# A searched instruction order keeps less of the source's order at its front

## The chip, the core and the metric

One core of a Trainium2 chip runs the program. The time is the device time of one execution in microseconds (us); lower is better. A core has five engines with an instruction queue each, which they work through in order: TensorE (PE in the profile; PEld are its weight loads), VectorE (DVE), ScalarE (ACT), GpSimd (POOL) and SyncE (SP), which here issues nearly all DMAs. The engines wait for each other by semaphores.

## What is computed

```python
xn = layernorm(x)                      # x: 1 x 2048 x 512
qkv = xn @ wqkv                        # 32 heads of 16
pq, pk = phi(q), phi(k)                # phi(t) = where(t > 0, t + 1, exp(t)) + 1e-6
kv = einsum("bhsd,bhse->bhde", pk, v); z = einsum("bhsd->bhd", pk)
o = einsum("bhqd,bhde->bhqe", pq, kv) / (einsum("bhqd,bhd->bhq", pq, z)[..., None] + 1e-6)
h = relu(xn @ w1 + b1) ** 2            # 1376 hidden columns
out = x + o @ wo + (h @ w2 + b2)       # float32
```

## The kernel before

The 2048 rows are 16 token tiles of 128 rows. A first loop over the tiles normalises each (xp), transposes it (PE for tiles 0 to 7, DVE after an exchange by DMA for the others), splits it into two parts whose sum is the float32 value (h and l: xs0h, xs0l for the transposed columns, tok for the rows), multiplies it with the k columns of wqkv (project, weights wkh and wkl), applies phi (k, then pk, again in two parts) and adds pk and the rows into four PSUM banks (kx). The names in the profile are those tiles, with their buffer numbers left out: st, mv and y are the statistics of the layernorm, t a transposed tile kept for DRAM. All later products are made of three passes of such parts.

After that two rounds (n = 0, 1) run over two blocks of 512 rows each. In each a loop makes the products with the columns of wqkv and w1 by a scheme of seven products instead of eight on half blocks (sums T of the rows, operands ops of the weights), evicts the PSUM banks (tiles rr, rf, h, more, by ACT copies and DVE additions), and then the second products with w2 and wo follow, whose left operands s are split by ACT and DVE just ahead. The operands of the weights are made in the first round from raw rows (raw), stored in DRAM (wd) and reloaded. At the end DVE transposes the results, adds them to x (res) and they are stored. There are four PSUM banks named ps and four named acc.

No instruction goes to an engine in the order of the source directly. A recorder (class Program) takes them as a list of 3188 tasks with their dependences. `order`, before anything is built, decides each engine's order by a search over its own cost table, and `emit` then writes the instructions out in the order of the planned starts. All instructions are written out at one line, L349, which is why the profile shows it for each.

Three lines set what the search may move. In `order`, an engine's fixed lane holds all of TensorE's tasks and, for other engines, those with an index below `nc.fixed`:

```python
self.lanes = {e: [t for t in ts if t.engine == e and (e == "tensor" or t.index < self.fixed)] for e in self.ENGINES}
...
for start in self.STARTS:
    chance, back = random.Random(start), (8, 16, 4)[start % 3]
```

A fixed lane is played in the source's order. After it, an engine takes of the tasks that are ready the one with the earliest due time. Each of the two starts in `STARTS` seeds a random generator; in 500 rounds the due times of tasks that led up to a planned TensorE wait are moved forward by random shares of it (`press`), the plan is played again, and the best is kept; `back` is after how many rounds without a gain the search returns to its best. The two results are then mixed by stretches of time. In the kernel's body `nc.fixed` is set after the recording of tiles 0 to 2's projections and of the first kx:

```python
kx(0)
nc.fixed = len(nc.tasks)
for i in range(2, NT):
```

The list holds 170 tasks at this point, the matmuls among them counted.

Of the kernel before, what the change touches and what calls it, by code (L numbers as in the profile page):

```python
# [79 lines left out]
class Program:  # L80
# [96 lines left out]

    ENGINES = ("tensor", "vector", "scalar", "gpsimd", "sync")
    DEEP, FAR = 4.0, 15.0
    STARTS = (6, 14)  # L180
    ROUNDS = 500

    def order(self):
# [36 lines left out]
        plain, best, found = [t.due for t in ts], None, []  # L220
        for start in self.STARTS:
            chance, back = random.Random(start), (8, 16, 4)[start % 3]
# [138 lines left out]
def kernel(  # L361
# [12 lines left out]
    nc = Program(tc.nc)  # L374
# [466 lines left out]
    def kx(i):  # L841
        order = (((1, 0),), ((0, 0), (0, 1))) if i >= NPE else (((0, 0),), ((0, 1),), ((1, 0),))
        todo = [(c, u, v) for group in order for c in range(NJ) for u, v in group]
        first, last = order[0][0], order[-1][-1]
        for c, u, v in todo:
            nc.tensor.matmul(kxp[c], lhsT=tok[i][:, u, c * P:(c + 1) * P], rhs=pk[i][:, v],
                             start=i == 0 and (u, v) == first, stop=i == NT - 1 and (u, v) == last)
# [394 lines left out]

    kxp = [bank(f"kx{c}", "acc") for c in range(NJ)]
    kx(0)
    nc.fixed = len(nc.tasks)
    for i in range(2, NT):
        if i == 3:
            nc.sync.dma_start(b1s[:, :NF - 1], b1[:(NF - 1) * P].rearrange("(f p) -> p f", p=P))
# [471 lines left out]
```

## Time and profile before

| | |
|---|---|
| median of 3 runs | 401.57 us (401.56 to 401.84) |
| profiled execution | 402.07 us |
| its span (first to last instruction) | 400.4 us |
| PE busy | 392.6 us, 98% |
| DVE, ACT, POOL busy | 353.5, 271.7, 49.5 us |
| granted TensorE clock | 0.997 of full |
| DMA | 94.37 MB, mean 236 GB/s |

The times of the stretches below are taken in the profiled execution, from its span's start. PE's matmuls are pipelined and their ends modelled in the profile, so "busy" can hide short gaps; a row of the timeline gives start, length, engine, line, operation, tiles out<-in, shapes, and in brackets the idle time of the engine just before with what ended it.

### The profile page before, as it was taken

Reading aid. Unit: us, or ns where it says so; the run is one execution under the profiler, and the core shown is the slowest. Engines: PE = TensorE matmul, PEld = TensorE weight load, DVE = VectorE, ACT = ScalarE, POOL = GpSimd, SP = SyncE. Lnnn points to the kernel's source line nnn. Section 1 sums busy time; section 2 is a strip of 40 time slices with the busy share of each in tenths; the row PEclk is TensorE's granted clock in tenths of the full one; section 3 lists DMA queues with packets and bytes.
Section 4 is the critical chain, followed back from the end, with each engine's and each line's share of the span. In section 5 each row is a group of like instructions: output and inputs, shape, how many; then the busy total and the mean of one; then the engine's idle time right before and its main releaser. Section 6 shows DMA issues by size and latency. Waiting matters only on the chain.

```text
span 400.4 us, 5611 instructions
## 1 busy us (share of the span) xinstructions
PE 392.6 (98%) x1763; PEld 324.5 (81%) x1763; DVE 353.5 (88%) x577; ACT 271.7 (68%) x478; POOL 49.5 (12%) x68
## 2 busy tenths in 40 slices
PE   7999999999999999999999999999999999999994
PEld 6778888888888887888888888887888888888884
DVE  5899999999998998999999999879999679676884
ACT  5786777677778989999757553186867677455440
POOL 2232322320122444100000000000000000000000
PEclk9999999999999999999999999999999999999998
DMA  7872387979678997797545799999975589999434
GB/s 235 289 220 58 94 249 229 338 283 310 248 230 306 327 359 275 250 315 262 186 146 199 245 235 243 306 250 255 272 232 185 178 226 292 227 281 278 156 64 95
DMA packets 80770, 94.37 MB, mean 236 GB/s; under 512 B 39490, under 2 KB 50754, under 8 KB 80484
## 3 DMA queue, kind: packets, MB, share of 16 engines
q1 hardware_dynamic: 79556, 93.49, 76.2%
q10 hardware_dynamic: 1088, 0.26, 0.3%
q0 software_dynamic: 96, 0.26, 0.3%
q8 instruction: 14, 0.23, 0.2%
q14 instruction: 16, 0.13, 0.1%
HBM read 57.81 MB, written 34.08 MB: 230 GB/s over the span
## 4 chain that ended last, share of the span: by engine, by line
PE 59%; DVE 1%; issue 0%
PE ps L349 32%; PE acc L349 28%; DVE res L349 0%; DVE o L349 0%
## 5 line engine op out<-in xcount | busy, mean ns | idle before, releaser
L349 PE MATMUL ps<-s,ops 128*128 128x512 f32 x435 | 102.6, 390 | 0.0
L349 PEld LDWEIGHTS ps<-s,ops 128*128 128x128 f32 x435 | 81.6, 188 | 17.1 <-ACT s L349 0.3
L349 DVE TENSOR_TENSOR s<-rr,s 128x512 fp32r<-128x512 f32 x56 | 38.2, 690 | 13.5 <-ACT s L349 12.9
L349 ACT ACTIVATE s<-rr 128x512 fp32r<-128x512 f32 x56 | 34.9, 630 | 22.2 <-DVE s L349 10.2
L349 PE MATMUL acc<-s,ops 128*128 128x512 f32 (+1 forms) x210 | 47.9, 380 | 0.0
L349 PE MATMUL acc<-pk,tok 128*128 128x512 f32 x192 | 47.1, 394 | 0.0
L349 PEld LDWEIGHTS acc<-s,ops 128*128 128x128 f32 x210 | 38.3, 188 | 7.5
L349 PEld LDWEIGHTS acc<-pk,tok 128*128 128x128 f32 x192 | 35.5, 188 | 7.8 <-DVE pk L349 0.6
L349 PE MATMUL acc<-T,ops 128*128 128x512 f32 x168 | 41.3, 390 | 0.0
L349 PE MATMUL ps<-T,ops 128*128 128x512 f32 x168 | 40.9, 391 | 0.1
L349 PEld LDWEIGHTS acc<-T,ops 128*128 128x128 f32 x168 | 31.5, 188 | 6.9 <-ACT rr L349 0.4
L349 PEld LDWEIGHTS ps<-T,ops 128*128 128x128 f32 x168 | 31.4, 188 | 7.0 <-ACT rf L349 0.5
L349 POOL DMA_DIRECT2D out_dram<-res x2 | 1.5, 728 | 229.0 <-DVE res L349 226.4
L349 POOL TENSOR_TENSOR tok<-xp,tok 128x512 fp32r<-128x512 f32 x16 | 21.7, 1354 | 42.1 <-ACT tok L349 30.6
L349 PE MATMUL ps<-xs0h,ops 128*128 128x512 f32 x72 | 23.7, 390 | 0.0
L349 ACT ACTIVATE rr<-acc 128x512 f32<-128x512 f32 x23 | 13.4, 586 | 12.3 <-PE acc L349 12.3
L349 DVE STREAM_TRANSPOSE d<-d 128x1024 f32<-128x1024 f32 x16 | 19.8, 1240 | 1.7 <-ACT d L349 1.5
L349 POOL TENSOR_TENSOR ops<-s,ops 128x512 fp32r<-128x512 f32 x12 | 15.9, 1328 | 25.3 <-ACT ops L349 22.2
L349 PE MATMUL acc<-xs0h,ops 128*128 128x512 f32 x56 | 18.4, 390 | 0.0
L349 ACT ACTIVATE s<-rf 128x512 fp32r<-128x512 f32 x19 | 11.9, 629 | 8.4 <-DVE rf L349 4.9
L349 ACT ACTIVATE rr<-rr,odds 128x512 f32<-128x512 f32 x15 | 10.8, 721 | 9.7 <-DVE rr L349 9.5
L349 DVE TENSOR_TENSOR ops<-raw,ops 128x512 fp32r<-128x512 f32 (+1 forms) x22 | 15.0, 681 | 2.6 <-ACT ops L349 2.6
(169 smaller groups left out, 801.4 us busy)
## 6 DMA issues: line engine op xcount, KB each, us to landing
ops<-wd SPq DMA_DIRECT2D x84, 256.0 KB, 4.1
wd<-ops SPq DMA_DIRECT2D x35, 512.0 KB, 3.6
ops<-wd SPq DMA_DIRECT2D x21, 512.0 KB, 5.8
wd<-ops SPq DMA_DIRECT2D x28, 256.0 KB, 3.5
res<-in_A_x_dram SPq DMA_DIRECT2D x32, 128.0 KB, 6.5
out_dram<-res SPq DMA_DIRECT2D x26, 128.0 KB, 3.6
ops<-wdz SPq DMA_DIRECT2D x6, 512.0 KB, 6.2
x<-in_A_x_dram SPq DMA_DIRECT2D x5, 512.0 KB, 4.9
```

What stands on the lines that cost most here:

```text
L349: getattr(getattr(self.nc, t.engine), t.name)(*map(real, t.args), **{k: real(a) for k, a in t.kw.items()})
```

## The change

`nc.fixed` becomes the constant 140. The tasks 140 to 169 of the list no longer keep the source's order: 12 of them are matmuls, which do so anyhow, and 18 belong to DVE (10), ACT (5), POOL (1) and SP (2). They are the end of the work on tiles 0 to 2: the roots and the normalisation of tile 3, phi and the parts of k of tile 1, the rows tok of tile 1, the statistics of tiles 8 and 9, and the loads of two raw blocks of w2. Besides, the two starts of the search are 0 and 9 instead of 6 and 14, with 8 and 8 as `back` instead of 8 and 4. Since both feed the search, the order of everything behind the first 140 tasks can differ on all engines but TensorE.

```diff
-    STARTS = (6, 14)
+    STARTS = (0, 9)
...
     kxp = [bank(f"kx{c}", "acc") for c in range(NJ)]
     kx(0)
-    nc.fixed = len(nc.tasks)
+    nc.fixed = 140
     for i in range(2, NT):
```

## Prediction

> **What bounds the kernel now.** I read the page first, then the busy time by stretches, then the chain, and only then the stretches at which the order changes. From the page:
>
> ```profile
> span 400.4 us, 5611 instructions
> PE 392.6 (98%) x1763; PEld 324.5 (81%) x1763; DVE 353.5 (88%) x577; ACT 271.7 (68%) x478; POOL 49.5 (12%) x68
> PEclk9999999999999999999999999999999999999998
> ```
>
> TensorE (PE) is busy for 98% of the span at the full granted clock. Where the other 2% lie, the busy time by stretches says (core 0: stretch, width, PE busy, weight loads, VectorE = DVE, ScalarE = ACT):
>
> ```profile
> 0.00:10.00 10.00, 7.88 (x38) 6.94 (x39) 5.78 (x18) 5.56 (x12) 2.55 (x15) 1.00 0.72 235
> 20.00:30.00 10.00, 9.76 (x47) 7.62 (x46) 9.16 (x24) 8.41 (x19) 3.94 (x7) 1.00 0.75 220
> 140.00:160.00 20.00, 19.90 (x88) 16.18 (x87) 17.68 (x28) 18.73 (x36) 8.71 (x8) 1.00 0.85 317
> 160.00:200.00 40.00, 40.00 (x178) 33.12 (x177) 39.10 (x62) 36.00 (x61) 1.30 (x1) 1.00 0.74 253
> 200.00:240.00 40.00, 40.00 (x178) 33.12 (x178) 38.89 (x63) 23.42 (x40) 0.00 (x0) 1.00 0.65 207
> 390.00:401.00 11.00, 5.08 (x31) 4.37 (x30) 4.51 (x9) 0.40 (x2) 0.69 (x2) 0.86 0.44 93
> sum 401.00, PE 392.61 PEld 324.55 DVE 353.50 ACT 271.73 POOL 49.48; mean PE 21.81 PEld 18.03 DVE 19.64 ACT 15.10 POOL 2.75
> ```
>
> Of 401.00 us PE idles 8.39: 2.12 in the first 10 us, 5.92 after its last matmul, 0.24 and 0.10 in the two stretches named; all others are full. The chain of waits ends so (start, length, what):
>
> ```profile
> 257.10 5.44 PE ps L349 x24
> ...
> 365.05 9.52 PE ps L349 x42
> ...
> 395.62 0.43 DVE res L349
> ```
>
> From 156 us on the chain is PE alone, up to the last transposes and additions. So the time is PE's fixed work, plus its waits, plus head and tail. PE's own order is not the search's: every matmul is placed by the source, and PE's order is the same in both kernels.
>
> **What can be won at all.** The head's order differs on no engine before 17.5 us, and the last 40 DVE, ACT and DMA instructions stand as before, so 2.12 and 5.92 stay. What is left is 0.24 + 0.10 = 0.34 us. The waits of the weight loads, which start ahead of the matmuls, give a far end (who waited for whom, us in total, times, longest):
>
> ```profile
> PEld acc L349 <- DVE pk L349: 0.6, 2, 0.3
> PEld ps L349 <- ACT rf L349: 0.5, 1, 0.5
> PEld acc L349 <- ACT rr L349: 0.4, 1, 0.4
> PEld ps L349 <- ACT s L349: 0.3, 1, 0.3
> ```
>
> Together 1.8 us. A gain lies between 0.34 and 1.8 us even if every one of these went; 0.2% of 401.57, about what a measurement of this kernel can tell from no change, is 0.80.
>
> The rows above give 5.44/24 = 0.227 and 9.52/42 = 0.227 us a matmul, in stretches that differ in what else runs: PE's pace does not hang on the order. The Trainium skill (Perfetto Trace Analysis, Identifying the Most-Contended Engine) warns that matmul busy time hides idle PE and wants weight-load busy time instead, which is 81% here; and TensorE: Matmul & The Clock Gate (Wait — 56ns, not 53.3ns?) gives 215.7 ns for a 512-column matmul. By these some 11 ns x 1600 = 18 us, an estimate, would be open to a better order. The even 0.227 speaks against that: the sum leaves it out, and of the faster rival's chance below 0.01 is for it.
>
> **Part 1, the front (18 to 27 us).** Freed are 18 instructions outside PE (140 to 169 of the list): x normalised for token tile 3 (xp), k and pk of tile 1, tok1, statistics, two weight loads from DRAM. DVE and ACT of before there (PE: who waits):
>
> ```profile
> 18.41 0.55 DVE L349 TENSOR_SCALAR xp<-x,mv,y 128x512 f32<-128x512 f32 x1
> 18.95 0.69 DVE L349 SCALAR_TENSOR_TENSOR k<-ps,k 128x512 f32<-128x512 f32 x1
> 19.55 0.68 DVE L349 BATCH_NORM_STATS2 st<-x 128x6 f32<-128x512 f32 x1
> 25.88 0.55 DVE L349 TENSOR_SCALAR xp<-x,mv,y 128x512 f32<-128x512 f32 x1
> ...
> 18.82 0.61 ACT L349 ACTIVATE tok<-xp 128x512 fp32r<-128x512 f32 x1
> 19.67 0.63 ACT L349 ACTIVATE pk<-k 128x512 fp32r<-128x512 f32 x1 [0.24 <-DVE k L349]
> 23.27 0.20 ACT L349 ACTIVATE y<-y 128x3 f32<-128x3 f32 x1
> 23.36 0.62 ACT L349 ACTIVATE tok<-xp 128x512 fp32r<-128x512 f32 x1
> ...
> 19.93 0.60 PE L349 MATMUL ps<-ident,xp 128*128 128x128 f32 x4
> 20.36 3.16 PE L349 MATMUL acc<-pk,tok 128*128 128x512 f32 x12
> ...
> 26.49 0.66 PE L349 MATMUL ps<-ident,xp 128*128 128x128 f32 x4 [0.24 <-DVE xp L349]
> ```
>
> The order on DVE there, before and then now (y, st, mv: statistics; x4: tile 5's too):
>
> ```order
> L349 SCALAR_TENSOR_TENSOR pk0_263<-k0_242,pk0_263 128x512
> L349 SCALAR_TENSOR_TENSOR y3_273<-mv3_229,y3_273 128x1
> L349 SCALAR_TENSOR_TENSOR y3_273<-y3_273 128x1 x2
> L349 TENSOR_SCALAR xp0_154<-x2_133,mv3_229,y3_273 128x512
> L349 SCALAR_TENSOR_TENSOR k1_279<-ps2_69,k1_279 128x512
> L349 BN_STATS st4_260<-x8_239 128x6
> ```
>
> Now:
>
> ```order
> L349 SCALAR_TENSOR_TENSOR pk0_263<-k0_242,pk0_263 128x512
> L349 BN_STATS st5_282<-x4_167 128x6
> L349 SCALAR_TENSOR_TENSOR y3_273<-mv3_229,y3_273 128x1
> L349 SCALAR_TENSOR_TENSOR y3_273<-y3_273 128x1 x2
> L349 SCALAR_TENSOR_TENSOR k1_278<-ps2_69,k1_278 128x512
> L349 TENSOR_SCALAR xp0_154<-x2_133,mv3_229,y3_273 128x512
> L349 BN_STATS st4_260<-x8_239 128x6
> ```
>
> A BN_STATS and k come ahead of xp. A 0.69 us step is followed after 0.60 (18.95 to 19.55), so xp moves by 2 x 0.60 = 1.2, to 19.61, and ends at 20.16. PE, free for its transposes at 19.93, waits until about 20.2: 0.3 us. On ACT a 0.58 us k comes between tok and pk, so pk moves from 19.67 to about 19.9; its matmuls, at 20.36 and now 20.66, still find it. At 26.49 PE had waited 0.24 for the next xp. If that xp comes no later, PE, 0.3 late, no longer waits, and 0.06 is left. But on ACT the y that it needs now stands behind tok (23.36) instead of ahead, 0.6 later, and DVE's use of that y ahead of statistics that used to fill the time; then xp would be up to 0.6 late, and since PE waited for it already, all of that is lost. Ends: a gain of 0.24 (no wait at 20, none at 26.49), a loss of 0.6. I take a loss of 0.3, what the rows at 18 to 20 us give.
>
> **Part 2, ACT at 132 to 137 us.** Both random starts of the search differ, so everything later is ordered anew. I looked for PSUM banks that PE gets back late. The rows with the least slack:
>
> ```profile
> 132.13 0.71 ACT L349 ACTIVATE e<-rr,odds 128x512 f32<-128x512 f32 x1
> 132.94 0.60 ACT L349 ACTIVATE rf<-ps 128x512 f32<-128x512 f32 x1
> 134.31 0.60 ACT L349 ACTIVATE rr<-ps 128x512 f32<-128x512 f32 x1 [0.24 <-PE ps L349]
> 135.84 0.59 ACT L349 ACTIVATE rf<-ps 128x512 f32<-128x512 f32 x1
> 136.84 0.72 ACT L349 ACTIVATE h<-h,odds 128x512 f32<-128x512 f32 x1
> ...
> 136.83 1.52 PE L349 MATMUL ps<-T,ops 128*128 128x512 f32 x6
> ```
>
> ACT's order before, from the e of 132.13 to the h of 136.84 (e, h: MLP and phi work in SBUF; rf and rr copy a bank out), and then now:
>
> ```order
> L349 ACTIVATE e_1450<-rr0_1_1314,odds_105 128x512
> L349 ACTIVATE rf2_1456<-ps3_70 128x512
> L349 ACTIVATE ops_1464<-s2_3_1453 128x2x256
> L349 ACTIVATE rr0_1_1314<-ps1_68 128x512
> L349 ACTIVATE ops_1475<-s4_3_1461 128x2x256
> L349 ACTIVATE rr0_1_1314<-rr0_1_1314 128x512
> L349 ACTIVATE rf2_1456<-ps0_67 128x512
> L349 ACTIVATE ops_1490<-raw_1_4_1259 128x2x256
> L349 ACTIVATE h2_1433<-h2_1433,odds_105 128x512
> ```
>
> Now:
>
> ```order
> L349 ACTIVATE e_1445<-rr0_1_1309,odds_105 128x512
> L349 ACTIVATE e_1450<-rr0_1_1309,odds_105 128x512
> L349 ACTIVATE h2_1434<-h2_1434,odds_105 128x512
> L349 ACTIVATE rf2_1464<-ps3_70 128x512
> L349 ACTIVATE ops_1470<-s2_3_1453 128x2x256
> L349 ACTIVATE rr0_1_1309<-ps1_68 128x512
> L349 ACTIVATE ops_1481<-s4_3_1461 128x2x256
> L349 ACTIVATE rr0_1_1309<-rr0_1_1309 128x512
> L349 ACTIVATE rf2_1464<-ps0_67 128x512
> ```
>
> A second e and the h now stand ahead of the copy of bank ps0 (135.84 to 136.43), which PE needs at 136.83: 0.40 of slack. They put 0.71 + 0.72 = 1.43 in its way; ACT's idle 0.10 before 132.94 and 0.24 before 134.31 take up 0.34. The copy ends 1.09 later, PE is 1.09 - 0.40 = 0.7 late against before. Lateness is not added up: PE's 0.3 from the front is part of it, since an ACT that is the later one no longer waits for PE. So this place adds 0.4, between 0 (if half the two fills other gaps) and 0.7 (if the front cost nothing).
>
> **Part 3, all the rest.** The same copy one round of the loop later:
>
> ```profile
> 153.35 1.14 ACT L349 ACTIVATE s<-rr 128x512 fp32r<-128x512 f32 x2
> ...
> 155.48 0.59 ACT L349 ACTIVATE rf<-ps 128x512 f32<-128x512 f32 x1
> ...
> 156.13 1.66 PE L349 MATMUL ps<-T,ops 128*128 128x512 f32 x6
> ```
>
> It had 0.06 of slack (156.07 to 156.13), and one more 0.6 us instruction stands ahead of it now, while the two s (1.14) moved to an earlier place. The ends are a gain of 0.3 and a loss of 0.7. In 160 to 240 us DVE idles 0.90 + 1.11 = 2.0 us in 80, so what DVE loses there beyond that goes to PE. DMA issues change places on SP only by a few ranks (0.4 us each), with PE microseconds away; I put them at nothing, and at up to 1 us if a reload of ops comes behind such a store. For all of it I take 0.5, ends -0.3 and 2.0, nearest to the 0.6 of one instruction out of place.
>
> **The sum.** 0.3 + 0.4 + 0.5 = 1.2 us. The profiled execution took 402.07 us, 1.67 beside its span, which stays; 403.27. The median of the three runs is 0.50 below that execution: 402.77, so 402.8, 0.3% slower.
>
> **The rivals.**
> *Slack takes it up.* PE meets no wait over 0.8 us in all, because the front's loss is given back at 26.49 and ACT's extra 1.43 finds other gaps. For it: 0.34 us of waits in a run of 390 us that this search left before. Against it: 0.40 and 0.06 of slack. Price +0.4: 402.0. Chance 0.26.
> *Faster.* The freed order brings the xp of 26.49 by 26.25 and the copies of 136 and 156 no later than before; then PE never waits behind the front. Price: 0.34, with the weight loads' waits some 1.0, so 400.6. It decides if that xp ends before 26.25 instead of 26.43; the rows above put it later. Chance 0.05.
> *Knock-on.* DVE loses more than the 2.0 us that it idles in 160 to 240, say by waiting for ACT with its own work queued behind, and PE waits for the operands s one product after another: 1.2 + 2.0 = 3.2 us, 404.8. It decides from 2.0 us of lost DVE time. Chance 0.14. The Trainium skill (TensorE: Matmul & The Clock Gate, Why this matters for your kernels) adds that PE gaps over some 3 us halve its clock. The clock row shows none at gaps of 0.24, and no wait here comes near 3.
> That the change moves nothing is out: the order shows it moved.
>
> **How the numbers follow.** Forecast 0.55, the rivals 0.26, 0.05, 0.14. Slower by over 0.2%: 0.55 + 0.14 = 0.69; within: 0.26; faster: 0.05. The range reaches from 401.2 (a gain of the 0.34) to 404.8 (knock-on): it leaves out the faster case and the worse half of the knock-on.
>
> **What would show it.** Right: PE waits of 0.3 near 20 us for DVE xp and of about 0.4 to 0.7 near 137 us for ACT rf; head, tail and the 0.227 us pace as before; about 1.2 us more PE idle between 10 and 395 us. Wrong: no new PE wait over 0.3 us, a tail other than 5.92 us, or a wait of over 2 us at one place, above all for a DMA.

## The result and the profile after

| | before | after |
|---|---|---|
| median of 9 runs each | 401.63 us (401.44 to 403.31) | 403.01 us (402.46 to 404.75) |
| ratio, 95% interval | | 1.0035 [1.0019, 1.0051] |
| profiled execution, its span | 402.07, 400.4 | 403.75, 402.0 |

The change made the kernel 1.38 us slower by the medians; 402.8 and a range of 401.2 to 404.8 had been forecast. Here and below, medians, ranges and ratios leave out executions more than 1.5% above the fastest of their kernel: one of the other starts alone (408.22 us), and two of the kernel with the y step later (568 and 666 us, at granted clocks of 0.66 and 0.56). The page of after begins:

```profile
span 402.0 us, 5615 instructions
PE 393.2 (98%) x1763; PEld 324.9 (81%) x1763; DVE 355.2 (88%) x577; ACT 271.8 (68%) x478; POOL 50.9 (13%) x68
```

The same engines are as busy as before, and PE has the same 1763 matmuls in the same order. So most of the 1.6 us of span should be waits of PE. These are the waits of PE in the whole span (who waited for whom, us, times, longest):

```profile
PE ps L349 <- DVE xp L349: 1.5, 2, 0.8
PE ps L349 <- DVE odds L349: 1.1, 1, 1.1
PE acc L349 <- ACT rr L349: 0.7, 1, 0.7
PE acc L349 <- DVE y L349: 0.2, 1, 0.2
```

The odds and y rows lie in the first 10 us. New are 1.5 for xp and 0.7 for rr. The busy time by stretches puts them in two stretches (columns as in the prediction's rows):

```profile
20.00:30.00 10.00, 8.48 (x41) 6.73 (x41) 9.41 (x23) 6.06 (x14) 3.39 (x5) 1.00 0.77 211
140.00:160.00 20.00, 20.00 (x90) 16.57 (x89) 18.93 (x29) 19.40 (x36) 10.12 (x8) 1.00 0.80 294
240.00:280.00 40.00, 39.30 (x173) 32.01 (x172) 35.00 (x47) 19.48 (x30) 0.00 (x0) 1.00 1.06 252
```

PE idles 1.52 us in 20 to 30 (before 0.24), 0 in 140 to 160 (before 0.10) and 0.70 in 240 to 280 (before 0). A wait can also stretch a group of matmuls without leaving a gap, so the surer reading is to set each matmul of after against the same one of before. Their starts differ by 0.04 at 17.28, so the head moved nothing; then by 1.03 at the transposes of 19.93, 0.86 at 23.36, 1.31 at 26.49, 1.27 at 136.83, 0.88 at 157.62, and 1.67 at 272.11 and to the end. The change costs 1.31 at the front, gives back 0.4 at 156 us and costs 0.8 at 273 us.

**The front.** The timeline of after there, PE, DVE and POOL:

```profile
20.96 0.66 PE L349 MATMUL ps<-ident,xp 128*128 128x128 f32 x4 [0.82 <-DVE xp L349]
27.80 0.66 PE L349 MATMUL ps<-ident,xp 128*128 128x128 f32 x4 [0.70 <-DVE xp L349]
...
18.94 0.68 DVE L349 SCALAR_TENSOR_TENSOR k<-ps,k 128x512 f32<-128x512 f32 x1
19.54 1.37 DVE L349 TENSOR_SCALAR xp<-x,mv,y 128x512 f32<-128x512 f32 x1
24.50 0.93 DVE L349 SCALAR_TENSOR_TENSOR y<-mv,y 128x3 f32<-128x3 f32 x1
...
19.33 1.30 POOL L349 TENSOR_TENSOR tok<-xp,tok 128x512 fp32r<-128x512 f32 x1 [1.87 <-ACT tok L349]
22.86 2.56 POOL L349 TENSOR_TENSOR tok<-xp,tok 128x512 fp32r<-128x512 f32 x2 [1.07 <-ACT tok L349]
```

The xp of tile 3 starts at 19.54 (19.61 was forecast) but takes 1.37 us instead of the 0.55 it took before. It ends at 20.91, 0.28 after POOL's tok (19.33 + 1.30 = 20.63). The little y step, 0.14 us before, takes 0.93 and ends with POOL at 25.42. Theory P is that these DVE instructions are held while POOL's TENSOR_TENSOR runs; its rival O is that only their later place counts.

**273 us.** DVE, ACT and PE of before, then of after:

```profile
255.11 0.69 DVE L349 TENSOR_TENSOR res<-o,res 128x512 f32<-128x512 f32 x1 [1.63 <-DMA res<-in_A_x_dram]
257.70 1.18 DVE L349 TENSOR_TENSOR T<-xT,T 128x1024 fp32r<-128x1024 f32 x1
271.48 0.58 ACT L349 ACTIVATE rr<-acc 128x512 f32<-128x512 f32 x1
272.11 1.65 PE L349 MATMUL acc<-T,ops 128*128 128x512 f32 x6
```

```profile
256.90 1.29 DVE L349 TENSOR_TENSOR res<-o,res 128x512 f32<-128x512 f32 x2 [2.30 <-DMA res<-in_A_x_dram]
258.74 1.19 DVE L349 TENSOR_TENSOR T<-xT,T 128x1024 fp32r<-128x1024 f32 x1
271.37 0.72 ACT L349 ACTIVATE e<-rr,odds 128x512 f32<-128x512 f32 x1 [0.91 <-DVE rr L349]
273.14 0.58 ACT L349 ACTIVATE rr<-acc 128x512 f32<-128x512 f32 x1
273.78 1.67 PE L349 MATMUL acc<-T,ops 128*128 128x512 f32 x6 [0.70 <-ACT rr L349]
```

PE waits for ACT's copy. Two things differ: in ACT's order an e that waits for DVE now stands ahead of a copy (theory S), and DVE, whose chain of e and rr leads to the copies, had stood still for a load of res 17 us earlier, 2.30 us instead of 1.63 (theory D).

### The profile page after: what moved, and what is told of

It reads as the page before. It is cut to its first block, busy times and chain, and to the rows that moved or that the text cites. A ratio compares the mean times of both kernels' runs of the same rounds, so it can differ in the third digit from the quotient of the medians.

```text
span 402.0 us, 5615 instructions
## 1 busy us (share of the span) xinstructions
PE 393.2 (98%) x1763; PEld 324.9 (81%) x1763; DVE 355.2 (88%) x577; ACT 271.8 (68%) x478; POOL 50.9 (13%) x68
## 4 chain that ended last, share of the span: by engine, by line
PE 89%; DVE 6%; ACT 2%; issue 1%; DMA 1%; DVEq 0%
PE ps L349 53%; PE acc L349 37%; DVE st L349 1%; DVE rr L349 1%; DVE o L349 1%; DMA x<-in_A_x_dram 1%; DVE xp L349 1%; ACT d L349 1%; DVE T L349 1%; DVE y L349 0%; ACT rr L349 0%; DVE res L349 0%; ACT e L349 0%; DVE k L349 0%; ACT k L349 0%
## 5 line engine op out<-in xcount | busy, mean ns | idle before, releaser
L349 PE MATMUL ps<-s,ops 128*128 128x512 f32 x435 | 102.6, 389 | 0.0
L349 PEld LDWEIGHTS ps<-s,ops 128*128 128x128 f32 x435 | 81.6, 188 | 17.2 <-ACT s L349 0.3
L349 DVE TENSOR_TENSOR s<-rr,s 128x512 fp32r<-128x512 f32 x56 | 39.1, 707 | 13.7 <-ACT s L349 13.1
L349 ACT ACTIVATE s<-rr 128x512 fp32r<-128x512 f32 x56 | 34.8, 630 | 20.7 <-DVE s L349 10.2
L349 PE MATMUL acc<-s,ops 128*128 128x512 f32 (+1 forms) x210 | 47.9, 380 | 0.0
L349 PE MATMUL acc<-pk,tok 128*128 128x512 f32 x192 | 46.9, 393 | 0.0
L349 PEld LDWEIGHTS acc<-s,ops 128*128 128x128 f32 x210 | 38.3, 188 | 7.6
L349 PE MATMUL acc<-T,ops 128*128 128x512 f32 x168 | 41.4, 391 | 0.7 <-ACT rr L349 0.7
L349 PEld LDWEIGHTS acc<-pk,tok 128*128 128x128 f32 x192 | 35.5, 188 | 7.6 <-DVE pk L349 0.3
L349 PE MATMUL ps<-T,ops 128*128 128x512 f32 x168 | 40.8, 390 | 0.0
L349 PEld LDWEIGHTS acc<-T,ops 128*128 128x128 f32 x168 | 31.4, 188 | 7.8 <-ACT rr L349 1.4
L349 PEld LDWEIGHTS ps<-T,ops 128*128 128x128 f32 x168 | 31.5, 188 | 6.5
L349 POOL DMA_DIRECT2D out_dram<-res x2 | 1.5, 726 | 229.5 <-DVE res L349 227.0
L349 POOL TENSOR_TENSOR tok<-xp,tok 128x512 fp32r<-128x512 f32 x16 | 22.0, 1380 | 39.5 <-ACT tok L349 33.5
L349 PE MATMUL ps<-xs0h,ops 128*128 128x512 f32 x72 | 23.6, 389 | 0.0
L349 ACT ACTIVATE rr<-acc 128x512 f32<-128x512 f32 x23 | 13.4, 589 | 14.1 <-PE acc L349 14.0
L349 DVE STREAM_TRANSPOSE d<-d 128x1024 f32<-128x1024 f32 x16 | 19.7, 1236 | 1.1 <-ACT d L349 0.9
L349 POOL TENSOR_TENSOR ops<-s,ops 128x512 fp32r<-128x512 f32 x12 | 17.5, 1469 | 24.2 <-ACT ops L349 24.2
L349 PE MATMUL acc<-xs0h,ops 128*128 128x512 f32 x56 | 18.4, 389 | 0.0
L349 ACT ACTIVATE s<-rf 128x512 fp32r<-128x512 f32 x19 | 12.0, 630 | 8.7 <-DVE rf L349 5.0
L349 ACT ACTIVATE rr<-rr,odds 128x512 f32<-128x512 f32 x15 | 10.8, 720 | 9.5 <-DVE rr L349 9.5
L349 PEld LDWEIGHTS ps<-xs0h,ops 128*128 128x128 f32 x72 | 13.5, 188 | 2.8
```

The lines of the kernel that those rows point to most:

```text
L349: getattr(getattr(self.nc, t.engine), t.name)(*map(real, t.args), **{k: real(a) for k, a in t.kw.items()})
```

## The experiments

Each kernel is the changed one, or the one before, with one edit. Instructions are moved in `emit`, on the list that the search returns, by task numbers; nothing else in the orders differs. The added lines shift the one line of all instructions from L349 to L354 to L359. Times are medians of 10 to 12 runs, ratios are to the kernel before in the same session.

### The halves of the change

```diff
-    STARTS = (0, 9)
+    STARTS = (6, 14)
```

> The freed order alone: 140 tasks kept, the starts still 6 and 14. On DVE the order of the front is now statistics of tile 4, the y of tile 3, xp, and only then k. Theory P (an xp or y of DVE is stretched when a TENSOR_TENSOR of POOL runs beside it, as the 1.37 us xp beside POOL's 1.30 us tok in the changed kernel): only one 0.6 us step stands ahead of xp, so it starts near 19.0, 0.3 before POOL's tok at 19.3, and runs 0.6 to 1.3 us; PE waits 0 to 0.7 at 20 us. Rival O (only its place in the row counts): xp ends near 19.6 and PE waits for nothing at 20 us. The wait of 0.70 at 273 us comes from the search's other result and need not be there. Time between the two kernels: 401.6 to 402.8.

403.12 us, ratio to before 1.0022 [1.0011, 1.0034]. That is over what was expected, and by the median as slow as the whole change, by another way. Its front costs nothing: xp, started at 18.79 ahead of POOL's tok at 19.07, takes 0.55, and PE's transposes of 26.49 come 0.20 earlier than before, as its matmul of 17.28 did (0.23). Then PE waits in a place where neither kernel does:

```profile
166.68 1.67 PE L349 MATMUL ps<-T,ops 128*128 128x512 f32 x6 [1.10 <-ACT rf L349]
```

PE loses 1.6 us there, and 1.0 more in 276 to 300 us, behind two short waits for ACT.

```diff
-    nc.fixed = 140
+    nc.fixed = len(nc.tasks)
```

> The other starts alone: 170 tasks kept, starts 0 and 9. The front stands as in the kernel before, so both theories expect the waits of before there: 0 to 0.1 for xp at 20 us, 0.2 at 26.5. ACT's copies at 270 us stand as before too. Both theories: the waits of the changed kernel at 20, 27 and 273 us (0.82, 0.70, 0.70) are gone, and 401.3 to 402.2 us; above 402.6 would say that the starts themselves carry the loss, by waits elsewhere.

403.92 us, 1.0057 [1.0032, 1.0081], with runs from 402.03 to 407.30. The front is that of before, as expected (0.26 for xp at 26.7), but the rest is worse than in either kernel. So the starts alone do carry a loss, which the expectation held for the less likely; but the two halves don't add up to the change, since each gives the search another problem and it returns another order for the whole run. Most of the loss of this one, in the profiled execution (407.30), is at 258 to 278 us. DVE and PE there, and then the busy time by stretches (a row ends with the granted clock, the DMA share and GB/s):

```profile
258.10 0.69 DVE L349 TENSOR_TENSOR res<-o,res 128x512 f32<-128x512 f32 x1 [3.64 <-DMA res<-in_A_x_dram]
273.09 2.63 PE L349 MATMUL acc<-T,ops 128*128 128x512 f32 x6 [2.14 <-ACT rr L349]
```

```profile
272.00:274.00 2.00, 0.91 (x3) 0.78 (x4) 0.90 (x2) 2.00 (x5) 0.00 (x0) 0.86 1.01 393
274.00:276.00 2.00, 2.00 (x7) 1.54 (x6) 1.29 (x2) 1.38 (x4) 0.00 (x0) 0.50 1.11 262
```

The load of res comes later still, the wait for ACT's rr grows to 2.14 us, and behind it the clock is granted by half: six matmuls take 2.63 us instead of 1.52. Against before PE is 4.01 us late at the matmul of 269.41 and 5.53 at that of 271.27: 1.5 us by the clock, on top of the wait.

### The front: place or POOL

```diff
+MOVES = ((144, "before", 147),)          # xp of tile 3 ahead of k, on DVE
...
-        for t in self.order() if reorder else self.tasks:
+        row = self.order()
+        for i, where, j in MOVES:
+            t = self.tasks[i]
+            row.remove(t)
+            row.insert(row.index(self.tasks[j]) + (where == "after"), t)
+        for t in row:
```

> The changed kernel with one DVE instruction moved: the xp of tile 3 stands ahead of k instead of behind it. P: xp starts near 18.9 instead of 19.54, runs mostly ahead of POOL's tok (19.33), takes 0.6 to 0.9 instead of 1.37 us, and PE's wait at 20 us falls from 0.82 to 0 or 0.1; k, behind it, may be the one that is held. O: xp ends 0.6 earlier, since k took 0.6, and PE still waits 0.2. The waits at 27 and 273 us (0.70 each) may grow by what is saved here, since PE comes there earlier: total 0 to 0.8 us less than the changed kernel.

402.44 us, 1.0007 [0.9995, 1.0019]. DVE, POOL and PE:

```profile
19.21 0.55 DVE L355 TENSOR_SCALAR xp<-x,mv,y 128x512 f32<-128x512 f32 x1
19.48 1.42 POOL L355 TENSOR_TENSOR tok<-xp,tok 128x512 fp32r<-128x512 f32 x1 [1.88 <-ACT tok L355]
21.07 3.01 PE L355 MATMUL acc<-pk,tok 128*128 128x512 f32 x12 [0.34 <-ACT pk L355]
```

xp, first by 0.27, runs its 0.55 us, and now POOL's tok takes 1.42 instead of 1.30. PE no longer waits for xp, but for pk, whose k was put back (0.34, not foreseen).

```diff
+MOVES = ((151, "after", 153),)           # POOL's tok of tile 1 behind pk
+        self.tasks[151].engine = "vector"
```

> The changed kernel with POOL's TENSOR_TENSOR tok of tile 1 (19.33, 1.30 us) done by DVE instead, behind pk and so behind xp: POOL is idle while xp runs, and xp keeps its place behind k. P: xp starts at 19.54 as in the changed kernel, but takes 0.55 us, and PE's wait for it falls from 0.82 to 0.1 or less. O: xp still takes 1.37 and PE waits 0.8. DVE gets some 0.7 us more to do before the y of 24.5, so the wait at 27 us may grow; the total says little here, the row does: 402.2 to 403.6.

402.39 us, 1.0008 [0.9993, 1.0023]. This one decides between P and O: xp keeps its place and its start.

```profile
19.54 0.54 DVE L356 TENSOR_SCALAR xp<-x,mv,y 128x512 f32<-128x512 f32 x1
23.80 1.14 DVE L356 SCALAR_TENSOR_TENSOR y<-mv,y 128x3 f32<-128x3 f32 x1
23.63 1.30 POOL L356 TENSOR_TENSOR tok<-xp,tok 128x512 fp32r<-128x512 f32 x1 [0.29 <-ACT tok L356]
20.14 0.66 PE L356 MATMUL ps<-ident,xp 128*128 128x128 f32 x4
```

With POOL idle beside it xp takes 0.54 us from the very start at which it had taken 1.37, and PE does not wait. O is out. The y step, beside the next tok, is held again until POOL's end (23.80 + 1.14 = 24.94; 23.63 + 1.30 = 24.93), and with it PE's second wait, 1.02 here.

```diff
+MOVES = ((182, "before", 183),)          # y's first step behind the statistics, on DVE
```

> The changed kernel with one DVE instruction moved: the first step y<-mv,y (128x3, 24.50, 0.93 us there) stands behind the two statistics, just ahead of the next step on y, so that POOL's tok (until 25.42) is over when it starts. P: it takes 0.14 us, no other step is held in its place, the xp behind it ends about 0.7 earlier, and PE's wait near 27.5 us falls from 0.70 to 0.1 or less; the wait at 20 us stays 0.82. O (the step is long for another reason, or xp is late by its place alone): it still takes 0.9 and PE waits 0.7. PE comes to 273 us about 0.7 earlier, and what is lost there may grow by as much, since the last res transfer comes when it comes: total 0 to 0.7 less than the changed kernel.

402.06 us, 1.0007 [0.9989, 1.0025].

```profile
25.99 0.14 DVE L355 SCALAR_TENSOR_TENSOR y<-mv,y 128x3 f32<-128x3 f32 x1
27.17 0.66 PE L355 MATMUL ps<-ident,xp 128*128 128x128 f32 x4
```

POOL is done by then: 0.14 us, and the second wait of PE is gone while the first (0.84) stays. P again. Last, the hold is made in the kernel before:

```diff
+MOVES = ((144, "after", 148),)           # kernel before: xp behind k and the statistics
```

> The kernel before with one DVE instruction moved: the xp of tile 3 stands behind k and the statistics, so that it comes at about 19.6, just after POOL's TENSOR_TENSOR tok has begun (19.51 to 20.79). P: xp takes 1.3 to 1.5 us instead of 0.55 and ends at about 21.05; PE, free for it at 19.93, waits 1.1. O: xp takes 0.55, ends at 20.15, PE waits 0.2. Of this some 0.2 may be given back at 26.5, where the kernel before waits 0.24. Total by P 0.6 to 1.2 more than the kernel before, by O 0 to 0.2 more.

402.63 us, 1.0024 [1.0009, 1.0038].

```profile
20.00 0.92 DVE L355 TENSOR_SCALAR xp<-x,mv,y 128x512 f32<-128x512 f32 x1
19.36 1.28 POOL L355 TENSOR_TENSOR tok<-xp,tok 128x512 fp32r<-128x512 f32 x1 [2.14 <-ACT tok L355]
20.97 0.66 PE L355 MATMUL ps<-ident,xp 128*128 128x128 f32 x4 [1.07 <-DVE xp L355]
```

xp came 0.4 later than expected (k waited 0.57 for ACT), so it was held for less, but it ends near where P said (21.05): at 20.92, again 0.28 after POOL's end (20.64). PE waits 1.07, and the total, 0.8 over the kernel before, lies where P had it, though some of it may be the load of res (below).

### 273 us: the order of ACT or the load of res

```diff
+MOVES = ((2250, "before", 2234),)        # the copy rr<-acc ahead of e, on ACT
```

> The changed kernel with one ACT instruction moved: the copy rr<-acc that PE waits for at 273 us stands ahead of the e that waits 0.91 for DVE, as in the kernel before. Theory S (ACT's order makes the loss): the copy comes 0.6 earlier, 272.5 instead of 273.14, and PE loses 0.1 to 0.2 there instead of 0.77. Theory D (DVE's wait of 2.30 us for a res transfer at 254.6 sets when the whole chain of e, rr and the copies comes): the copy that PE waits for still hangs on e, and PE loses 0.5 to 0.8. Front as in the changed kernel. Total by S 0.6 less than the changed kernel, by D the same to 0.2 less.

402.59 us (402.20 to 404.73), 1.0020 [1.0005, 1.0036]. The total decides nothing: it is 0.42 under the changed kernel, between the two expectations, and the intervals overlap. In its profile PE loses nothing at 273 us, but that tells nothing either: the load of res happened to come early in that execution.

```profile
254.69 1.30 DVE L355 TENSOR_TENSOR res<-o,res 128x512 f32<-128x512 f32 x2 [0.28 <-DMA res<-in_A_x_dram]
```

The profiles of the earlier experiments tell more, since SP's order is the same in all of them and the load came at a different time in each:

```profile
256.38 1.30 DVE L355 TENSOR_TENSOR res<-o,res 128x512 f32<-128x512 f32 x2 [1.98 <-DMA res<-in_A_x_dram]
```

```profile
255.09 1.30 DVE L356 TENSOR_TENSOR res<-o,res 128x512 f32<-128x512 f32 x2 [0.95 <-DMA res<-in_A_x_dram]
```

```profile
255.67 1.30 DVE L355 TENSOR_TENSOR res<-o,res 128x512 f32<-128x512 f32 x2 [1.50 <-DMA res<-in_A_x_dram]
```

These are xp first, tok on DVE and y later. Take from each time by how much PE is late against before just ahead (the matmul of 157.62: 0.69, 0.43, 0.29; the changed kernel 0.88), and set it against what PE lost from there to behind the group of 272.11 (the matmul of 273.60) more than the kernel before did:

| | DVE goes on at | less PE's lateness | PE lost more than before |
|---|---|---|---|
| changed kernel | 256.90 | 256.02 | 0.81 |
| xp first | 256.38 | 255.69 | 0.47 |
| y later | 255.67 | 255.38 | 0.16 |
| tok on DVE | 255.09 | 254.66 | -0.33 |

(The 0.77 of the expectations is the 0.81, counted from a slightly earlier matmul.) ACT's order is the same in the four, and S alone would have them lose the same. The loss follows the load of res one for one: 0.33 earlier and 0.34 less, 0.31 earlier and 0.31 less. The last row loses nothing at all, and the kernel before a third of a microsecond (below, it gains 0.35 there without its wait for res). Nor does the old order of ACT protect from a late load: in the profile of the kernel before with the late xp (404.76 us, the slowest of its runs) the load came later still, and PE lost 1.94 us, 1.30 of them as the wait shown:

```profile
257.81 0.69 DVE L355 TENSOR_TENSOR res<-o,res 128x512 f32<-128x512 f32 x1 [3.55 <-DMA res<-in_A_x_dram]
260.40 1.18 DVE L355 TENSOR_TENSOR T<-xT,T 128x1024 fp32r<-128x1024 f32 x1
274.18 0.58 ACT L355 ACTIVATE rr<-acc 128x512 f32<-128x512 f32 x1
271.67 1.66 PE L355 MATMUL acc<-T,ops 128*128 128x512 f32 x6 [1.30 <-ACT rr L355]
```

So D holds. S has a part in it, which DVE's order hides. Once the load is late, the copy that PE needs for the group of 272.11 starts 14.40 us after DVE's T step in the changed kernel (258.74 to 273.14; 14.41 with xp first and with y later), but 13.78 after it in the two kernels with the old order (257.70 to 271.48, 260.40 to 274.18): the e ahead of the copies costs 0.62. In the same change a transposition of DVE moved from behind the wait for res to ahead of it, so the T step follows the wait after 1.84 instead of 2.59 us. The two nearly cancel. The next edit takes the load away as a cause:

```diff
+MOVES = ((2079, "after", 2076), (2080, "after", 2079), (2081, "after", 2080))   # on SP
```

> The changed kernel with three DMA issues moved on SP: the loads of res for the second token tile (needed 15 us later) stand behind those of the first, for which DVE waits 2.30 us at 254.6. They are 128 KB each; at the 303 GB/s of that stretch the first tile's last load lands some 1.3 us earlier. D: DVE's wait falls to about 1.0, the chain of e and copies comes 1.3 earlier, and PE's loss of 0.77 at 273 us is gone, though ACT's order there stays as it is. S: the loss stays 0.6 or more. If SP had been waiting for the first tile's buffer rather than for the queue, the last landing does not move and nothing changes. Total by D 0.5 to 0.8 less than the changed kernel.

402.39 us, 1.0008 [0.9997, 1.0019], and all twelve runs between 402.24 and 402.64, where the changed kernel's lie between 402.46 and 404.75. DVE, ACT and PE:

```profile
254.45 1.25 DVE L355 TENSOR_TENSOR res<-o,res 128x512 f32<-128x512 f32 x2
271.87 0.58 ACT L355 ACTIVATE rr<-acc 128x512 f32<-128x512 f32 x1
272.71 1.54 PE L355 MATMUL acc<-T,ops 128*128 128x512 f32 x6
```

DVE doesn't wait at all, the copy is there 0.26 us ahead of PE, and nothing is lost though the e still stands ahead of the copy. So S is out as the cause: without the late load ACT's order costs nothing at 273 us.

```diff
 # the kernel before
+        late = [t for t in row if t.index in (2079, 2080, 2081)]      # res of the second token tile
+        row = [t for t in row if t not in late]
+        last = max(k for k, t in enumerate(row) if t.index in range(2071, 2079))
+        row[last + 1:last + 1] = late                                 # behind res of the first
```

> The kernel before with the same three loads moved on SP, nothing else. D: DVE's wait for res (1.63 in the profile of before) is what spreads the runs of the kernel before from 401.3 to 403.5; without it all runs come to 401.3 to 401.7, the lowest of before, and the median is 0.1 to 0.4 under that of before. S: median and spread as before.

401.52 us (401.37 to 401.77), 0.9987 [0.9976, 0.9998]: the lowest runs of the kernel before, all the time.

```diff
 # the other starts alone (170 tasks kept), with the same four lines
```

> The other starts alone (170 tasks kept), now with the three res loads moved. With the starts alone PE lost 3.0 us by waits for ACT rr at 269 to 273 us and some 1.5 more by the clock granted behind them (0.50 at 274 to 276 us), in runs of 402.0 to 408.2. D: all of that is gone, the clock stays full, and 402.0 to 402.6 is left in every run, with the 0.7 us that this order loses at 96 us. S: the waits stay.

402.18 us (401.91 to 402.66), 1.0003 [0.9994, 1.0012]. The wait of 2.14 us is gone and with it the half clock: the clock row of its page stands at full.

### Put together

```diff
+MOVES = ((144, "before", 147), (182, "before", 183))
 # and the four lines for res
```

> The changed kernel with three edits at once: xp of tile 3 ahead of k, the y step behind the statistics, and the three early loads of res for the second token tile behind those of the first. If the loss is the two holds by POOL and the res transfer, nothing of it is left but the 0.34 us by which pk comes late when xp goes first: 401.5 to 402.0, and as narrow a spread as with the res loads alone (0.4 us from the lowest to the highest run, where the changed kernel has 2.3). If something else carries a part, 402.3 or more.

401.38 us (401.27 to 401.55), 0.9981 [0.9971, 0.9992]. The causes found leave nothing of the loss: it is 0.14 under the kernel before with the same loads moved (401.52, same session), and a little better than expected, since the 0.4 us gained at 156 us are kept.

```diff
+LAST_OF_FRONT = 378
...
+        row = self.order()
+        self.STARTS, self.fixed = (6, 14), 170
+        front = self.order()
+        front = front[:[t.index for t in front].index(LAST_OF_FRONT) + 1]
+        row = front + [t for t in row if t not in front]
 # and the four lines for res
```

> The changed kernel with its front put back: on all engines the tasks up to the second kx (29 us) in the order of the kernel before, all behind it as in the changed kernel, and the three res loads moved. Waits at 20, 27.5 and 273 us are gone; what the changed kernel gained at 156 us (0.35 less there than before) stays. 401.0 to 401.4, 0.1% under the kernel before, and a narrow spread. If the rest of the changed order loses something that the front's lateness hid (the copy rf<-ps at 137 us, predicted to be 0.7 late), a PE wait for ACT rf shows there, and the total is 401.6 or more.

401.16 us (401.00 to 401.43), 0.9977 [0.9969, 0.9986]: faster than both kernels. Three kernels with narrow spreads now divide the change. The order behind the front gains 401.52 - 401.16 = 0.36; the front costs 402.39 - 401.16 = 1.23; together 0.87. The 402.39 is from another session than the other two, but the profiles agree: against before, from 17.28 to 96 us, PE gets 1.25 later with the new front and 0.00 with the old one. The medians of the two kernels differ by 1.38; what is left, 0.5, would be what the load of res costs the changed kernel more than the one before. That remainder is not shown: the changed kernel was measured in one session only, and the median of the kernel before went from 401.63 to 402.05 over the four.

## Why the prediction came out right, point by point

The time was right, its terms were less so: the front cost four times what it was given (1.3 for 0.3), the term at 137 us nothing (for 0.4), the rest 0.4 (for 0.5). That an error of 1.0 too little and one of 0.4 too much left the sum within the range is luck. So is part of the agreement of the medians, 1.2 forecast and 1.38 measured: the two profiled executions differ by 1.7. Of the signs, a wait for xp near 20 us came, at 0.82 for 0.3, and PE idles 1.9 us more in 10 to 395 us (for 1.2); the one for rf near 137 us did not come; and a wait of over 2 us for a DMA, named as a sign of being wrong, did, though on DVE (2.30).

**What bounds the kernel.** Right: PE's work and its order did not change, head and tail moved nothing, and the whole loss is PE's waits. The page of the Trainium skill named there (Perfetto Trace Analysis, Identifying the Most-Contended Engine) calls matmul busy time a poor measure of how near PE is to its peak, since pipelined matmuls look smaller in a trace; that idle PE hides in it is the prediction's reading. Here it hid 0.6 us: PE is busy 393.2 us instead of 392.6 with the same matmuls.

**Part 1, a loss of 0.3 with ends of -0.24 and 0.6.** The mechanism was right (xp behind BN_STATS and k, at 19.61), the size was not: 1.31 in the profile, 1.23 between the kernels, twice the far end. The step that failed is "and ends at 20.16": it gave the moved xp the 0.55 us of its old place. At its new place it ran beside POOL's tok and took 1.37. The row that would have shown this was in the trace of before, a step away from those quoted, the pk of tile 1 beside the same tok:

```profile
20.37 0.97 DVE L349 SCALAR_TENSOR_TENSOR pk<-k,pk 128x512 fp32r<-128x512 f32 x1
19.51 1.28 POOL L349 TENSOR_TENSOR tok<-xp,tok 128x512 fp32r<-128x512 f32 x1 [2.14 <-ACT tok L349]
```

With POOL idle the same pk takes 0.67 in the changed kernel. Nor was the wait at 26.49 given back; there the y step was held too, and PE waited 0.70.

**Part 2, 0.4 near 137 us.** Wrong: no wait. With the old front, so that no lateness from the front covers it, ACT and PE of the order behind stand so:

```profile
135.50 0.59 ACT L359 ACTIVATE rf<-ps 128x512 f32<-128x512 f32 x1
136.48 1.52 PE L359 MATMUL ps<-T,ops 128*128 128x512 f32 x6
```

The slack is 136.48 - 136.09 = 0.39, as before the change (0.40). That the e and the h are more work ahead of the copy is right, and ACT's busy time in the 17.84 us up to the copy's start says so, before and in the changed kernel (stretch, width, busy times; the fourth of these is ACT's):

```profile
118.00:135.84 17.84, 17.84 (x80) 14.79 (x79) 15.76 (x25) 15.53 (x29) 7.44 (x7) 1.00 0.84 292
119.27:137.11 17.84, 17.84 (x80) 14.78 (x79) 16.40 (x27) 16.81 (x31) 6.97 (x7) 1.00 0.87 294
```

The step that failed is the idle time set against them: "0.10 before 132.94 and 0.24 before 134.31", 0.34. It began to count at 132.13. From 118 us on ACT had 17.84 - 15.53 = 2.31 us idle; the search put one more e there (122.47), and 1.03 are left: the 1.28 that went took up the two, and the copy stands no later against PE.

**Part 3, 0.5 for the rest.** Right in the size of the sum, 0.8 - 0.4 in the profile, and in neither of its parts. The copy at 155.48, given a gain of 0.3 or a loss of 0.7, was a gain of 0.4. The loss came from the loads on SP, which the prediction put "at nothing, and at up to 1 us if a reload of ops comes behind such a store": it was the loads of res, between which the reloads stand. The words "with PE microseconds away" leave out DVE, which stood still for the load and was late with all its work behind it, up to the copies 17 us later. Whether SP's new order makes the load later, or only the execution that was profiled, is not shown: the kernel before went on at 255.11 in one profile, and at 257.81 with the late xp and the same order on SP.

**Lateness is not added up.** Right in kind: at 273 us PE loses less the later it comes.

**The rivals.** Slack did not take the front's loss up, but it did take ACT's extra work up, as that rival had it. The knock-on (DVE waits with its own work queued, PE waits behind it, 404.8) is there as a mechanism, for a load instead of ACT: in the profile of 404.76 us above, and with the other starts alone. The changed kernel's slowest run (404.75) comes to the same time, but has no profile. The faster kernel was not this one; the new order with the old front gains the 0.34 that this rival was priced at (0.36).

## What to carry to other kernels

When an order moves an instruction, its time at the new place is not that of the old: look up what runs beside it there, for DVE whether POOL does, and set added work against the engine's idle time ahead of the first row that differs too, not only behind it. A wait on an engine that works in order is paid by all behind it, even 17 us later. Where the runs of one kernel spread, look for the load on which they wait: moving three loads took the spread of the changed kernel from 2.3 us to 0.4, and the medians of both kernels were lower with it.

## What was not expected of the hardware

DVE's TENSOR_SCALAR with its source in SBUF (xp) and its two-operand steps with both in SBUF (pk, y) are held while POOL's TENSOR_TENSOR runs, and end 0.28 us (xp, twice), 0.55 us (pk) or 0.01 us (y, twice) after POOL does, whenever they began; the other way round POOL's tok took 1.42 for 1.30. BN_STATS (0.68 beside tok) and k, with an operand in PSUM (0.68, with xp first all of it beside tok), are not held. The Trainium skill (SBUF — State Buffer, SBUF: two separate sides) says the same: the port pair that DVE and GpSimd share is locked for a whole instruction by whoever starts first, for DVE in a mode that uses two ports or with two SBUF inputs. This case agrees that the two exclude each other, if not for the whole length: tok lost only 0.12 us when xp was still busy for 0.28 of it. The prediction weighed two rules of TensorE's pace and clock and missed this one, which spoke against the change.

A PE wait of 2.14 us, behind one of 0.29, was followed by a granted clock of 0.50 and cost 1.5 us more; behind the waits of 0.70, 0.82, 1.07, 1.10 and 1.30 us shown above it stayed at 1.00. The Trainium skill (TensorE: Matmul & The Clock Gate, Why this matters for your kernels) puts the limit at some 3 us, and the prediction's knock-on relied on it; this trace shows it lower, at least once.

The load of res let DVE go on at 254.7 to 256.9 us in five profiles with the same SP order, while the DMA engines were full (share 1.16 in 240 to 250 us of the changed kernel). What makes the difference is not shown:

```profile
240.00:250.00 10.00, 10.00 (x46) 8.29 (x45) 9.97 (x13) 3.80 (x5) 0.00 (x0) 1.00 1.16 221
```
